# Linear attention, Fourier mixing and feed-forward in one kernel: the check's flag is loaded in the middle, and a PSUM layout is turned

## The chip, the cores and the metric

The kernel runs on one core of one Trainium2 chip. A time is the device time of one execution in microseconds; the number for a kernel is the median of its runs. Engines are named as in the profile: PE is TensorE (PEld its weight loads), DVE is VectorE, ACT is ScalarE, POOL is GpSimd, SP is SyncE. A "q" behind an engine's name marks an instruction of its sequencer (a wait, a branch, the issue of a transfer).

## The reference

Four batches, eight heads, 768 tokens, 48 features per head. First a gated linear attention, token by token, and then, on the heads side by side (384 features), a Fourier mixing over tokens and features, a normalization and a two-layer feed-forward with a residual:

```python
for t in range(S):
    state = alpha[:, :, t, :, None] * state + np.einsum('bhd,bhe->bhde', k[:, :, t], v[:, :, t])
    y[:, :, t] = np.einsum('bhd,bhde->bhe', q[:, :, t], state)
...
X = np.fft.fft(x, axis=1)
X = np.fft.fft(X, axis=2)
u = x + np.real(X)
un = (u - mean(u)) / np.sqrt(var(u) + 1e-06)
out = u + np.maximum(un @ w_ch1, 0.0) @ w_ch2
```

## The kernel before, in words

**Two paths.** The fast path works on chunks of 128 tokens and divides by running products of `alpha`. This needs products that stay in range, so it also makes a check: each pair of heads leaves a count in `bad` (ScalarE, stage `s1`) and six chunk products in `over`. At the end `lim`, `bs` and a one-column product on TensorE turn these into `fl`, an integer 0 or 1. A general path follows under `tc.If(flag > 0)` (line 1375): it computes the whole output again with a scan over each state column. With the inputs of the reference the flag is 0 and every engine jumps over it. Its code is large for some engines: `general_pair` and `general_rest` use PE, DVE, ACT and SP much, POOL little.

**The fast path's stages.** Each of the 16 pairs of heads (`attn_stages`, four pairs per batch) goes through `s1` to `s8`: two scans that make the running products and their inverses (`products`, which also copies the chunk products to `over` and to `fade_`), the multiplications with keys and queries, transposes of the keys (`s4`), scores (`s5`), the chunk states (`s6`), the output (`s7`) and the first step of the mixing (`s8`). In `s6` five chunks times two heads give ten products of 128x48 into one PSUM tile `pu`; VectorE multiplies them by the chunk products `mt` into `tc_`, where the chunk is the innermost index, a scan over the five chunks makes the states, and two ScalarE copies put them into `tt`. After four pairs comes the Fourier mixing of the batch: a token stage with twelve products per two groups (`token_stage`, which writes PSUM with a step of six), a feature stage, a gather through DRAM, and the normalization. The feed-forward (`ffn_stages`) has for each of two blocks of 384 tokens twelve slices, each with nine matmuls in and nine out, weights and data split into a high and a low part.

**What sets the order.** Nothing is emitted where it is written. Every instruction goes into a `Plan` (line 212) with a key (its due order), the engines that could do it (`FX`), and durations from `Plan.duration` (line 334). `Plan.emit` (line 398) places them greedily on modelled clocks and then emits the instructions in that order; almost all have line 530 in the profile (ScalarE's relu 249). Feed-forward matmuls have `fill` and take whatever time the others leave on TensorE. Where the plan leaves TensorE idle before the time `WARM`, `plan.idle` inserts dummy matmuls of 128x48 on `zero` (line 1284), one per 0.11 us of planned gap.

**The end of the program.** The check's instructions have the key `B * 1000`, behind everything. After `plan.emit()` line 1302 loads the flag into a register of every engine (`nc.values_load`), each waiting for `fl`; line 1375 is the branch, and line 1437 the close of the program, where SP waits for all engines and all transfers.

The input and output transfers of the fast path are issued by SP, two small ones by ACT, the gathers by POOL.

Of the kernel before, what the change touches and what calls it, by code (L numbers as in the profile page):

```python
# [17 lines left out]
ALU = mybir.AluOpType  # L18
AX = mybir.AxisListType

B, H, S, D = 4, 8, 768, 48
# [10 lines left out]
CW = 112  # L32
# [25 lines left out]
KFM = 40.0  # L58
WARM = 120.0
SWITCH = 0.09  # L60
# [151 lines left out]
class Plan:  # L212


    def __init__(self, engines):
        self.engines, self.ops, self.tags, self.direct, self.key, self.chain, self.fill = engines, [], {}, None, 0.0, None, False
        self.idle, self.open, self.both, self.half, self.tight = None, set(), None, None, False
        self.read = {}

# [33 lines left out]
    def add(self, engines, name, args, kwargs):  # L253
        engine = engines[0]
        fns = {e: self.method(e, name) for e in engines}
# [78 lines left out]
    def duration(self, op, named, engine):  # L334
        n = op.free
        if "dma" in op.name:
            return 1.05 if engine == "POOL" else 0.05
        if engine == "PE":
            m = self.region(named["1"])[4]
            if op.name == "transpose":  # L340
                return max(m, self.region(named["2"])[4]) / 1200 + 0.002
            if str(named["1"].real(self.base(named["1"])).dtype).endswith("float32"):
                slow = 1.65 if self.stride(named["2"]) > 16 else 1.0
                p0, p1 = self.region(named["1"])[0:2]
                return max(m, slow * n) / (750 if p1 - p0 <= GRP else 600) + 0.004
            return n / 2240 + 0.003
        if engine == "ACT":
            pointer = 0.094 if any(isinstance(named.get(k), View) for k in ("bias", "scale")) else 0.0
            slow = 1.8 if self.stride(named["out"]) > 16 and n > 64 else 1.0
            return (0.11 if self.psum(named.get("1")) else 0.14) + slow * n / 1200 + pointer + (0.25 if "accum_out" in named else 0.0)  # L350
        if op.name == "memset":
            return n / (960 if engine == "DVE" else 1100) + 0.01
        if engine == "DVE":
            if op.name == "bn_stats":
                return 0.47
            if op.name == "reciprocal":
                return 0.07 + n / 160
            if op.name == "tensor_tensor_scan":
                return 0.1 + n / 480
            if isinstance(named.get("scalar1"), View):  # L360
                return 0.09 + n / 1200
            whole = "bitcast" in [s[0] for s in named.get("out", View(None)).steps]
            pointer = 0.06 if isinstance(named.get("scalar"), View) else 0.0
            return 0.09 + pointer + n / (1920 if whole and op.name == "tensor_scalar" else 960)
        return 0.126 + n / 1094 if op.name == "affine_select" else 0.15 + n / 477

    def stride(self, view):

        ap = view.real(self.base(view))
        return abs(ap.ap[-1][0]) * mybir.dt.size(ap.dtype)  # L370

    def port(self, op, named):
# [25 lines left out]
    def emit(self):  # L398
# [33 lines left out]

        placed = 0
        while placed < len(ops):
# [32 lines left out]
            t, n, engine = best  # L467
            op = ops[n]
            for e in op.engines:
                wait[e].remove(n)  # L470
# [26 lines left out]
            if "dma" in op.name:  # L497
                dge = max(dge, t) + 0.47
                wire = max(wire, dge + 0.6) + op.wire * (1.4 if wire < 9.0 else 0.9)
                end = wire + 1.0  # L500
            op.t, op.end = t, end
            order.append(n)
            for slot in op.slots:
# [7 lines left out]
            for m in op.users:  # L511
                u = ops[m]
                u.left -= 1
                for e in u.engines:
# [4 lines left out]
                    if not u.left:  # L519
                        wait[e].append(m)  # L520
        self.order = [n for n in order if isinstance(n, int)]
        for n in order:
# [27 lines left out]
def gla_mix_ffn(ctx: ExitStack, tc: tile.TileContext, alpha, kq, v, w1, w2, consts, tables, rowtab, out):  # L550
# [172 lines left out]
    def attn_stages(b, hp, i, mixed):  # L723
# [83 lines left out]
        def s6():  # L807
            pu = psa()
            ea = tc_.rearrange("p (e a) -> p a e", a=NT - 1)
            for a in range(NT - 1):  # L810
                for hd, r in HEADS:
                    T.matmul(
                        pu[r, a * D : (a + 1) * D], e["kt"][:, a, r], loaded["vn", pair][:, (2 * a + hd) * D : (2 * a + hd + 1) * D],
                        start=True, stop=True,
                    )
            V.tensor_tensor(
                out=ea[0:CW], in0=pu[0:CW, 0 : (NT - 1) * D].rearrange("p (a e) -> p a e", e=D),
                in1=mt[0:CW, 0 : NT - 1, None].broadcast_to([CW, NT - 1, D]), op=ALU.mult,
            )
# [430 lines left out]
    for b in range(B):  # L1250
# [14 lines left out]
        if b + 1 < B:  # L1265
# [6 lines left out]
            write(mixing(), b * 1000 + KM)  # L1272
    plan.key = B * 1000.0
    lim, wide = bad[0:CW, B * NP2 :], over[0:CW]
# [4 lines left out]
    T.matmul(pf[0:1, 0:1], bs, ones, start=True, stop=True)  # L1279
    V.tensor_scalar_min(fl, pf[0:1, 0:1], 1.0)  # L1280
    warm = {tag: plan.tags[tag]["reals"] for tag in ("f2", "f1")}
    if WARM:
# [18 lines left out]
    plan.direct = own  # L1301
    flag = nc.values_load(fl.real()[0:1, 0:1], min_val=0, max_val=1)
    ydram = dp.tile([B * NP2, S, 2 * D], F32, name="ydram")
# [70 lines left out]

    with tc.If(flag > 0):
        with tc.tile_pool(name="gp", bufs=1) as pool:
# [64 lines left out]
```

## Time and profile before

| | |
|---|---|
| median of 3 runs | 508.88 us (508.25 to 509.34) |
| the profiled execution: its time | 508.06 us |
| its span, first to last instruction | 506.3 us |
| mean granted TensorE clock | 0.996 |
| HBM read, written | 37.69 MB, 7.08 MB |

A row of grouped instructions has line, engine, operation, out<-in by the program's names (buffer numbers left out), shapes and count, then busy time, mean ns of one, and the idle time of the engine before them with what ended it. A row of the timeline has start, duration, then the same. A row of one line's instructions has count, duration ns (minimum/median/maximum), and first and last start. The ends of matmuls are modelled, so rows of matmuls overlap.

### The profile page before, as it was taken

To read this page: it belongs to the slowest core of one execution; us is meant where nothing else is said; L and a number is where in the kernel's file an instruction comes from. 1 tells how busy PE (TensorE), PEld (TensorE's weight loads), DVE (VectorE), ACT (ScalarE), POOL (GpSimd) and SP (SyncE) were. 2 spreads that over 40 slices of the span, in tenths; PEclk is the share of its full clock that TensorE was granted. 3 is DMA by queue.
4 is the path that set the end of the run, shared out by engine and by line. 5 is a ranking of instruction groups with operands and counts; after the bars stand their busy time and mean duration, and the time that the engine had idled before them with its cause. 6 is when DMAs were issued, how large, how long until landed. Compare 5 with 4: busy or idle time off the path is not lost.

```text
span 506.3 us, 9559 instructions
## 1 busy us (share of the span) xinstructions
PE 495.9 (98%) x3956; PEld 472.8 (93%) x3956; DVE 322.6 (64%) x617; ACT 206.9 (41%) x417; POOL 61.9 (12%) x76
## 2 busy tenths in 40 slices
PE   9999999999999999999999999999999999999993
PEld 8888769999999999999999999999999999999993
DVE  8999989999789996561799516661648214113111
ACT  3494678576664164544323314445123312111110
POOL 0000250532113002121200002121300000000000
PEclk9999999999999999999999999999999999999998
DMA  8993442234532103322431001200201001001001
GB/s 304 407 403 130 117 138 92 95 88 176 212 109 81 47 1 141 117 91 89 141 104 48 0 1 48 87 26 2 79 18 47 1 1 47 1 0 48 0 1 53
DMA packets 20978, 45.47 MB, mean 90 GB/s; under 512 B 1920, under 2 KB 11008, under 8 KB 20928
## 3 DMA queue, kind: packets, MB, share of 16 engines
q1 hardware_dynamic: 19872, 42.29, 23.8%
q0 software_dynamic: 768, 2.37, 1.7%
q8 instruction: 33, 0.54, 0.5%
q10 hardware_dynamic: 288, 0.13, 0.1%
q14 instruction: 17, 0.14, 0.1%
HBM read 37.69 MB, written 7.08 MB: 88 GB/s over the span
## 4 chain that ended last, share of the span: by engine, by line
PE 96%; DVE 2%; issue 0%
PE f L530 68%; PE a L530 24%; PE f L1284 4%; DVE y L530 1%; DVE st L530 0%; DVE r L530 0%; DVE mv L530 0%; DVE f L530 0%; DVE x L530 0%; DVE zero L530 0%; DVE fl L530 0%
## 5 line engine op out<-in xcount | busy, mean ns | idle before, releaser
L530 PE MATMUL f<-x,wt 128*128 128x384 f32 x864 | 178.6, 343 | 0.6 <-DVE x L530 0.6
L530 PE MATMUL f<-wt,h 128*128 128x384 f32 x864 | 176.5, 343 | 0.0
L530 PEld LDWEIGHTS f<-x,wt 128*128 128x128 f32 x864 | 150.7, 188 | 1.9 <-DVE x L530 0.8
L530 PEld LDWEIGHTS f<-wt,h 128*128 128x128 f32 x864 | 151.2, 188 | 1.3 <-issue 0.5
L530 DVE SCALAR_TENSOR_TENSOR h<-f,h 128x384 fp32r<-128x384 f32 x96 | 53.2, 554 | 110.2 <-ACT h L249 109.6
L249 ACT ACTIVATE h<-f 128x384 fp32r<-128x384 f32 x96 | 47.2, 492 | 169.3 <-PE f L530 154.9
L530 POOL TENSOR_SCALAR_AFFINE_SELECT w<-w 128x384 f32<-128x384 f32 x48 | 34.7, 746 | 208.1 <-ACT w L530 207.9
L530 PE MATMUL a<-vn,w 128*128 128x80 f32 x288 | 42.6, 270 | 0.0
L530 PEld LDWEIGHTS a<-vn,w 128*128 128x128 f32 x288 | 39.6, 191 | 0.6
L530 ACT COPY w<-a 128x384 f32<-128x384 f32 (+4 forms) x60 | 26.4, 482 | 26.2 <-PE a L530 25.0
L530 DVE TENSOR_TENSOR y<-y,a 128x191 f32<-128x191 f32 (+3 forms) x65 | 25.1, 427 | 10.4 <-PE a L530 10.4
L530 DVE TENSOR_TENSOR_SCAN w<-al,d 112x773 f32<-112x773 f32 (+1 forms) x17 | 28.7, 1691 | 4.6 <-PE a L530 3.4
L530 DVE TENSOR_TENSOR_SCAN al<-al,back 112x773 f32<-112x773 f32 (+1 forms) x17 | 30.0, 1762 | 0.2
L1284 PE MATMUL f<-zero 128*32 128x48 f32 x518 | 27.8, 212 | 1.1 <-DVE zero L530 1.1
L1284 PEld LDWEIGHTS f<-zero 128*32 128x32 f32 x518 | 24.5, 114 | 4.4 <-issue 1.5
L530 ACT COPY tt<-tc 64x240 f32<-64x240 f32 (+1 forms) x32 | 20.5, 640 | 12.1 <-DVE tc L530 11.6
L530 PEld LDWEIGHTS a<-w,al 64*128 64x128 f32 (+1 forms) x288 | 17.9, 187 | 5.1 <-ACT w L530 2.5
L530 PE MATMUL a<-w,al 64*128 64x128 f32 (+1 forms) x288 | 22.5, 288 | 0.0
L530 DVE TENSOR_TENSOR z<-y,y 128x576 f32<-128x576 f32 x16 | 12.8, 832 | 15.2 <-ACT y L530 15.1
L530 POOL DMA_INDIRECT y<-scr,rows x12 | 15.4, 1285 | 56.8 <-DMA scr<-y 32.0
L530 PE MATMUL a<-tt,w 112*128 112x96 f32 x120 | 21.4, 276 | 0.0
L530 ACT COPY y<-a 128x288 f32<-128x288 f32 x24 | 9.6, 402 | 25.8 <-PE a L530 25.8
(113 smaller groups left out, 545.3 us busy)
## 6 DMA issues: line engine op xcount, KB each, us to landing
kq<-in_kq_dram SPq DMA_DIRECT2D x13, 768.0 KB, 5.5
wt<-in_w_dram SPq DMA_DIRECT2D x8, 768.0 KB, 8.4
al<-in_alpha_dram SPq DMA_DIRECT2D x15, 388.0 KB, 5.7
out_dram<-y SPq DMA_DIRECT2D x24, 192.0 KB, 2.3
vn<-in_v_dram SPq DMA_DIRECT2D x14, 304.0 KB, 3.0
wt<-in_w_dram SPq DMA_DIRECT2D x8, 384.0 KB, 6.5
scr<-y SPq DMA_DIRECT2D x4, 577.5 KB, 4.7
wt<-in_kq_dram SPq DMA_DIRECT2D x2, 768.0 KB, 11.7
```

Source lines behind the costliest of these rows:

```text
L249: return lambda out, x: e.activation(out, x, AF.Relu)
L530: op.ins = op.fns[op.engine](*[real(a) for a in op.args], **{k: real(x) for k, x in op.kwargs.items()})
L1284: lambda tag, i: nc.tensor.matmul(warm[tag][i][0:32, 512 - FW : 512], zero.real()[:, 0:32], zero.real(), start=True, stop=True), 1.0, WARM,
```

## The change

Four things. The check's instructions get a key that lies within batch 2's work (2430), behind the attention of the last batch, and `Plan.emit` emits the load of the flag for all engines at the first instruction placed more than 10 us of planned time after `fl` is planned to be done. In the general path (`self.direct`) what SP issued is issued by ACT. In `s6` the products are written with the chunk innermost, so that PSUM, the multiplication's other operand and `tc_` have the same order. And the planner's prices change: TensorE's for products with at most 64 weight columns on full rows, ScalarE's for inputs with a step over 16 bytes and for outputs with a last dimension under 8; `WARM` goes from 120 to 220.

```diff
-WARM = 120.0
+WARM = 220.0
...
     def add(self, engines, name, args, kwargs):
-        engine = engines[0]
+        engine = "ACT" if self.direct and engines[0] == "SP" else engines[0]
+        engines = (engine,) if self.direct else engines
...
+                if m <= GRP < p1 - p0:
+                    return max(m / 2, n) / 600 + 0.004
                 return max(m, slow * n) / (750 if p1 - p0 <= GRP else 600) + 0.004
...
-            slow = 1.8 if self.stride(named["out"]) > 16 and n > 64 else 1.0
+            apart = max(self.stride(named[k]) for k in ("out", "1") if isinstance(named.get(k), View)) > 16
+            slow = 1.8 if (apart or self.short(named["out"])) and n > 64 else 1.0
...
+    def short(self, view):
+        ap = view.real(self.base(view)).ap
+        return len(ap) > 2 and ap[-1][1] < 8
...
+            if due is not None and t > due:
+                order.append(self.after)
+                due = None
...
+            if n == self.last:
+                due = end + 10.0
...
-                        pu[r, a * D : (a + 1) * D], e["kt"][:, a, r], loaded["vn", pair][:, (2 * a + hd) * D : (2 * a + hd + 1) * D],
+                        pu[r, a : (NT - 1) * D : NT - 1], e["kt"][:, a, r], loaded["vn", pair][:, (2 * a + hd) * D : (2 * a + hd + 1) * D],
...
-                out=ea[0:CW], in0=pu[0:CW, 0 : (NT - 1) * D].rearrange("p (a e) -> p a e", e=D),
-                in1=mt[0:CW, 0 : NT - 1, None].broadcast_to([CW, NT - 1, D]), op=ALU.mult,
+                out=tc_[0:CW].rearrange("p (e a) -> p e a", a=NT - 1), in0=pu[0:CW, 0 : (NT - 1) * D].rearrange("p (e a) -> p e a", a=NT - 1),
+                in1=mt[0:CW, None, 0 : NT - 1].broadcast_to([CW, D, NT - 1]), op=ALU.mult,
...
-    plan.key = B * 1000.0
+    plan.key = (B - 2) * 1000.0 + KA + 10.0
...
+    flag = []
+    plan.last = len(plan.ops) - 1
+    plan.after = lambda: flag.append(nc.values_load(fl.real()[0:1, 0:1], min_val=0, max_val=1))
...
-    flag = nc.values_load(fl.real()[0:1, 0:1], min_val=0, max_val=1)
...
-    with tc.If(flag > 0):
+    with tc.If(flag[0] > 0):
```

More of the change, by code (lines that the diff above doesn't have):

```diff
@@ L217, in __init__ @@
         self.idle, self.open, self.both, self.half, self.tight = None, set(), None, None, False
-        self.read = {}
+        self.read, self.last, self.after = {}, None, None
     def tag(self, name, count, make):
@@ L431, in finish @@
             return (max(t, held[other[e]]) if op.port and e in held else t) + op.durs[e]
-        placed = 0
+        placed, due = 0, None
         while placed < len(ops):
@@ L520, in emit @@
                         wait[e].append(m)
+        if due is not None:
+            order.append(self.after)
         self.order = [n for n in order if isinstance(n, int)]
```

## The prediction

> **What bounds the kernel now.** I read the page's totals first, then windows over four stretches, the end of the timeline, the sequencers' rows behind it, and last the groups that the change touches.
>
> ```profile
> span 506.3 us, 9559 instructions
> PE 495.9 (98%) x3956; PEld 472.8 (93%) x3956; DVE 322.6 (64%) x617; ACT 206.9 (41%) x417; POOL 61.9 (12%) x76
> PE 96%; DVE 2%; issue 0%
> ```
>
> TensorE carries 96% of the chain that ended last, but that averages over stages. Here are the windows (PE, PEld, DVE, ACT, POOL, then clock, DMA share, GB/s), and the dummy matmuls of line 1284 with their first and last start:
>
> ```profile
> 10.00:60.00 50.00, 49.49 (x572) 42.05 (x573) 48.52 (x82) 30.41 (x55) 3.64 (x3) 1.00 0.73 281
> 80.00:120.00 40.00, 40.00 (x317) 38.10 (x315) 37.94 (x55) 27.89 (x56) 10.91 (x9) 1.00 0.18 59
> 120.00:220.00 100.00, 100.00 (x781) 96.48 (x779) 80.19 (x149) 49.94 (x104) 15.04 (x20) 1.00 0.33 112
> 220.00:498.00 278.00, 278.00 (x1909) 272.30 (x1909) 130.11 (x275) 80.47 (x171) 22.43 (x31) 1.00 0.12 40
> L1284 PE MATMUL f<-zero x518: 206/206/288, 1.1 to 77.0; 128*32 128x48 f32 x173
> ```
>
> So there are three stages. Until 77 us TensorE is padded with dummies, and VectorE is the full engine (48.52 of 50 us between 10 and 60), with DMA at 0.73 beside it. From 80 to 498 us TensorE never stops: only a change in its own work counts there. The third stage is the end:
>
> ```profile
> 497.59 1.61 DVE L530 TENSOR_TENSOR y<-y,f 128x384 f32<-128x384 f32 x3 [1.03 <-PE f L530]
> 498.54 0.09 PEld L530 LDWEIGHTS a<-ones,bs 128*1 128x1 f32 x2 [0.25 <-issue]
> 498.54 0.19 PE L530 MATMUL a<-ones,bs 128*1 128x1 f32 x2
> 499.12 0.14 DVE L530 TENSOR_SCALAR fl<-a 1x1 int32<-1x1 f32 x1
> ```
>
> The last addition ends at 497.59 + 1.61 = 499.20 us, yet the span runs to 506.3. After the flag (499.26) no engine is busy; the sequencers' rows (q behind the engine; first and last start) show what is there:
>
> ```profile
> L1302 PEldq TENSOR_LOAD <-fl x1: 662/662/662, 499.3 to 499.3; - x1
> L1302 SPq TENSOR_LOAD <-fl x1: 981/981/981, 500.1 to 500.1; - x1
> L1375 SPq EVENT_SEMAPHORE  x8: 17/17/17, 504.1 to 504.7; - x8
> L1375 POOLq EVENT_SEMAPHORE  x2: 17/30/43, 500.2 to 500.3; - x2
> L1375 POOLq COMPARE_BRANCH  x1: 45/45/45, 500.0 to 500.0; - x1
> L1375 PEldq COMPARE_BRANCH  x1: 4462/4462/4462, 500.1 to 500.1; - x1
> L1375 SPq COMPARE_BRANCH  x1: 45/45/45, 501.5 to 501.5; - x1
> L1375 DVEq EVENT_SEMAPHORE  x1: 21/21/21, 503.6 to 503.6; - x1
> L1375 PEldq EVENT_SEMAPHORE  x1: 51/51/51, 504.6 to 504.6; - x1
> L1437 SPq EVENT_SEMAPHORE  x14: 17/28/28, 504.7 to 506.3; - x14
> L530 SPq DMA_DIRECT2D out_dram<-y x3: 534/575/582, 498.2 to 499.5; - x3
> DMA to landing us min/median/max: 2.2/2.4/2.7
> ```
>
> Every engine loads the flag after it is made (499.3), then jumps over the general path. The jump is long on engines with much code there: PE's takes 4.46 us, SP goes from its branch at 501.5 to its next instruction at 504.1 (2.6 us), DVE goes on at 503.6. POOL, with little code there, takes 0.2 us (500.0 to 500.2). SP comes last: its load stands behind its output transfers (500.1 to 501.1), then the branch, then eight releases from 504.1 to 504.7, and the closing run to 506.3. The last two rows say that the third output transfer starts at 499.5, keeps SP 0.58 us, and that these three land 2.4 us after their issue.
>
> **The tail, after the change.** The flag is made and loaded long before, so nobody loads at the end. SP has no transfers of the general path left (ScalarE has them), so I give its jump POOL's 0.2 us. The third output transfer lands at 499.5 + 2.4 = 501.9; SP, past its jump at 500.3, waits for that. From the last release to the end is 506.3 - 504.7 = 1.6 us; the landing is awaited somewhere among eight releases that take 0.6 us, so I add 0.3: the end is 501.9 + 1.6 + 0.3 = 503.8, a gain of 2.5 us. With the landing at its shortest, 2.2 us, and awaited last, the gain is 3.0. If SP's jump stays at 2.6 us, SP goes on at 500.1 + 2.6 = 502.7 instead of 504.1, and 1.4 us are gained.
>
> PE's 4.46 us jump must not become the end. Does PE's sequencer reach it early? A wait in the first stage answers:
>
> ```profile
> L530 PEldq EVENT_SEMAPHORE  x1: 2257/2257/2257, 26.7 to 26.7; - x1
> 27.38 1.34 PE L530 MATMUL f<-vn,x 128*128 128x80 f32 x10
> 28.65 0.27 PE L1284 MATMUL f<-zero 128*32 128x48 f32 x2
> ```
>
> From 26.7 to 29.0 PE's sequencer stood still while the array ran ten matmuls and two dummies that had been queued before. So it runs some 2 us ahead: it meets the branch 2 us before the last matmuls (498.5 - 2 = 496.5) and is through by 501.0, ahead of the landing. ScalarE's last work lies earlier than that. VectorE's 3.6 us (500.0 to 503.6), started no later than 499.2, ends by 502.8, about when SP asks for it. If PE did not run ahead, its jump would end at 498.7 + 4.5 = 503.2, and with the 1.7 us from there (504.6 to 506.3) the end would be 504.9: a gain of 1.4.
>
> **The flag inside the feed-forward.**
>
> ```profile
> L530 DVE TENSOR_SCALAR bad<-over x1: 407/407/407, 326.5 to 326.5; 112x96 f32<-112x96 f32 x1
> L530 DVE TENSOR_REDUCE bs<-bad x1: 270/270/270, 332.1 to 332.1; 128x1 f32<-128x112 f32 x1
> ```
>
> The sums were made at 326 to 332 us already; their new key changes little. What moves is the one-column product, the flag, and five loads. The product's two matmuls now stand in TensorE's full stretch: 0.19 us, or 0.44 with the 0.25 of issue that preceded them; I take 0.25. Behind it on PE wait feed-forward matmuls, and behind those the output. The load blocks PE's sequencer for 0.66 us; by the wait above the array has some 2 us queued, so it costs nothing. Without that cover it costs 0.66. On ACT, DVE and SP, loads of 0.65 to 0.98 us fall into a stretch where VectorE is busy 130 of 278 us: nothing, at worst the same 0.66 once. The queues passed on SP hold only transfers; POOL is idle.
>
> **Keys' products, chunk innermost.**
>
> ```profile
> L530 DVE TENSOR_TENSOR tc<-a,over 112x240 f32<-112x240 f32 x12 | 7.2, 598 | 17.6 <-PE a L530 17.6
> L530 DVE TENSOR_TENSOR tc<-f,over 112x240 f32<-112x240 f32 x4 | 2.3, 585 | 0.1
> L530 DVE TENSOR_TENSOR y<-y,a 128x191 f32<-128x191 f32 x36 | 11.2, 343 | 0.0
> L530 DVE TENSOR_TENSOR y<-y,a 128x384 f32<-128x384 f32 x24 | 12.7, 546 | 10.4 <-PE a L530 10.4
> 29.03 0.75 PE L530 MATMUL f<-wt,kt 128*64 128x48 f32 x20
> 26.35 0.60 PE L530 MATMUL f<-cst,al 112*128 112x112 f32 x4
> 60.31 2.68 PE L530 MATMUL f<-cst,h 128*97 128x65 f32 x24
> ```
>
> The multiplication wrote with a step of five and took 585 to 598 ns for 240 elements. Two others that read PSUM without such a step take 343 for 191 and 546 for 384, so 1.05 ns per element and 343 + 49 x 1.05 = 394 for 240: 0.2 us less, 16 times, 3.2 us of VectorE. Only the first four can shorten the time, in the stage where VectorE is full: at most 4 x 0.19 = 0.76. The matmuls that now write with a step of five (20 bytes) are the twenty of 0.75 us per pair. The token stage already writes with a step of six: twelve products (641 and 640 columns) in two passes each, 2562 columns in 2.68 us, 1.05 ns per column; four contiguous transposes, 448 columns in 0.60, are no faster. So I take nothing. As the upper bound, if the step held the keys' 960 columns to 1.05 ns each, though two heads now run beside each other, the twenty would take 1.0 us: 0.25 more, 3.0 for the twelve pairs in the full stretch.
>
> The Trainium skill, PSUM — Partial Sum Buffer, section Specifications (TRN2), speaks against this edit: it says that any non-contiguous access pattern in PSUM slows matmuls significantly. It gives no factor, and the token stage's row does not bear it out.
>
> **The planner's new prices.**
>
> ```profile
> L530 ACT COPY fade<-w 112x192 f32<-112x192 f32 x11 | 5.9, 540 | 0.0
> L530 DVE COPY fade<-w 112x192 f32<-112x192 f32 x4 | 1.4, 362 | 0.0
> ```
>
> They move no work by themselves, but the order is made anew. Dearer ScalarE copies may send some fades to VectorE: 0.36 us each, up to three more in the first stage, 1.1 us against the 0.76 saved. I take -0.3 for both together, from -0.8 to +1.1. In the full stretch the order can only cost stalls or save few: nothing, plus or minus 0.8. The dummies up to 220: before, none came after 77 us although 120 was allowed, so the plan had no gaps there; nothing, at most ten (10 x 0.05 = 0.5 us, since 518 took 27.8). The transfers issued by ScalarE are never run.
>
> **Sum**, on the profiled execution (span 506.3, its own time 508.06): tail -2.5, product +0.25, loads 0, matmuls' step 0, first stage -0.3, order and dummies 0: -2.55, so 505.5. The median of the runs, 508.88, lies 0.82 above that execution; the same -2.55 on it gives 506.3.
>
> **Rivals.**
>
> *Half the tail (chance 0.12).* SP's jump stays long, because what Tile itself puts on SP for the general path's loops is more than POOL's share; or the load is not hidden. A tail of 1.4 in place of 2.5 gives 507.4; a load of 0.66 on TensorE, 507.0; both, 508.1. For it: SP had 2.6 us, and no row shows how much of that was transfers. Against it: POOL has the same loops and jumps in 0.2. The Trainium skill, Runtime: NRT & Kernel Launch, section Instruction fetch mechanics, says that a taken branch stalls for a fetch only when its target lies outside the blocks already loaded; by it SP's rest must fit such a block, which no row here shows.
>
> *Nothing (0.07).* Something not seen, such as the code fetches themselves, sets the end wherever the flag is: 508.9. Against it: POOL's short jump at the same time.
>
> *Slower, by the new order in the first stage (0.10).* The first feed-forward matmul, near 77 us, waits for a chain through a full VectorE. If the new prices put another pair's two scans and a product ahead of it, everything behind moves:
>
> ```profile
> L530 DVE TENSOR_TENSOR_SCAN al<-al,back 112x773 f32<-112x773 f32 x15 | 28.0, 1869 | 0.1
> L530 DVE TENSOR_TENSOR al<-kq,al 112x768 f32<-112x768 f32 x13 | 12.3, 945 | 1.9 <-DMA kq<-in_kq_dram 1.9
> ```
>
> Two scans and one product are 4.7 us: 506.3 + 4.7 = 511.0. It decides from a delay of 2.6 us on. For it: VectorE has no slack there. Against it: the new prices are nearer to the measured ones (540 ns for the fade).
>
> *Slower, by the step in PSUM (0.05).* If the keys' matmuls take twice as long, the twelve pairs in the full stretch cost 12 x 0.75 = 9 us: 515.3. It decides from 1.3 times on.
>
> **How the numbers follow.** A measurement of this kernel can tell 0.2%, 1.0 us, from no change. The forecast has 0.66 and by its terms runs from 504.8 to 507.6. The range goes on to 508.9 and takes in half the tail and nothing; the two slower cases, 0.15, stay out. Faster by over 1.0 us: nearly all of the forecast, 0.63, and two thirds of half the tail, 0.08: 0.71. Slower: 0.05 and most of the other, 0.08: 0.13. The rest, 0.16, is the same.
>
> **What would show it.** Right: no load of the flag after the last matmul; PE's branch starting before its last matmul; SP's next instruction within 0.3 us of its branch; the last addition followed by 4.6 us (503.8 - 499.2) and not 7.1; the multiplication near 394 ns; the first feed-forward matmul within 1 us of 77. Wrong: a gap in PE's weight loads at the flag's load, dummies after 80 us, keys' twenty matmuls over 0.9 us, or SP's jump still at 2.6.

## The result, and the profile after

The changed kernel takes 513.63 us (median of 6 runs, 510.43 to 514.13) where the kernel before takes 508.94 (6 runs beside it, 508.25 to 509.34): ratio 1.0084, 95% interval 1.0057 to 1.011. It is slower by 4.7 us, and the forecast of 506.3 missed by 7.3.

The profiled execution took 513.36 us. Its span:

```profile
span 511.6 us, 9570 instructions
```

The windows over the same four stretches as before:

```profile
10.00:60.00 50.00, 49.82 (x573) 42.48 (x571) 44.52 (x76) 29.37 (x55) 2.46 (x2) 1.00 0.73 281
80.00:120.00 40.00, 40.00 (x318) 37.49 (x317) 38.41 (x60) 27.57 (x57) 11.12 (x9) 0.98 0.25 83
120.00:220.00 100.00, 99.23 (x766) 95.24 (x766) 78.94 (x146) 49.55 (x100) 14.34 (x20) 1.00 0.30 101
220.00:498.00 278.00, 277.97 (x1921) 272.13 (x1921) 133.77 (x280) 83.48 (x178) 23.11 (x33) 1.00 0.13 44
```

TensorE is as full as before, VectorE has less to do between 10 and 60 us (44.52 us, 48.52 before), and the stretch from 120 us on lacks little: one idle time of 0.8 us between 120 and 220. So the loss must lie at an end of the program. The last addition is the place to cut (timeline of after, its end):

```profile
503.69 1.61 DVE L545 TENSOR_TENSOR y<-y,f 128x384 f32<-128x384 f32 x3 [1.04 <-PE f L545]
```

It ends at 503.69 + 1.61 = 505.30 and ended at 499.20: 6.10 us later. From there to the end of the span it is 6.34 us instead of 7.14. So the tail gained 0.80, and 6.10 were lost ahead of it. The profile of before, around the first feed-forward matmul (f<-x,wt), first on GpSimd, then on VectorE, then on TensorE:

```profile
61.18 0.95 POOL L530 DMA_INDIRECT y<-scr,rows  x1 [0.30 <-issue]
66.01 3.60 POOL L530 TENSOR_TENSOR wt<-wt 128x768 f32<-128x768 f32 x2 [3.88 <-ACT wt L530]
69.57 3.61 POOL L530 TENSOR_TENSOR wt<-wt,wt 128x768 fp32r<-128x768 f32 x2
...
71.97 1.22 DVE L530 SCALAR_TENSOR_TENSOR r<-mv,r 128x3 f32<-128x3 f32 x1
...
73.82 0.48 DVE L530 TENSOR_SCALAR f<-y,r,r 128x384 f32<-128x384 f32 x1
...
74.64 1.20 PE L530 MATMUL f<-cst,f 128*128 128x128 f32 x9 [0.63 <-ACT f L530]
...
76.40 0.44 PE L530 MATMUL f<-x,wt 128*128 128x384 f32 x1
```

The same place in after:

```profile
63.49 4.69 POOL L545 DMA_INDIRECT y<-scr,rows  x1 [0.30 <-issue]
68.20 1.83 POOL L545 TENSOR_TENSOR wt<-wt,wt 128x768 fp32r<-128x768 f32 x1
69.97 3.59 POOL L545 TENSOR_TENSOR wt<-wt 128x768 f32<-128x768 f32 x2
73.50 3.58 POOL L545 TENSOR_TENSOR wt<-wt,wt 128x768 fp32r<-128x768 f32 x2
...
72.76 0.52 DVE L545 TENSOR_TENSOR y<-y,a 128x384 f32<-128x384 f32 x1
73.20 0.17 DVE L545 RECIPROCAL r<-r 128x3 f32<-128x3 f32 x1
73.42 3.69 DVE L545 SCALAR_TENSOR_TENSOR r<-mv,r 128x3 f32<-128x3 f32 x1
...
77.73 0.48 DVE L545 TENSOR_SCALAR f<-y,r,r 128x384 f32<-128x384 f32 x1
...
78.55 2.18 PE L545 MATMUL f<-cst,f 128*128 128x128 f32 x9 [3.09 <-ACT f L545]
80.67 1.17 PE L1302 MATMUL f<-zero 128*32 128x48 f32 x12
81.77 0.44 PE L545 MATMUL f<-x,wt 128*128 128x384 f32 x1
```

The first feed-forward starts at 81.77 instead of 76.40, 5.37 later, and three differences make that up. The three-element instruction r<-mv,r starts 73.42 - 71.97 = 1.45 later. It then takes 3.69 us instead of 1.22, 2.47 more, and ends (77.11) where GpSimd's last pair of subtractions ends (77.08); in before it ended (73.19) where that pair ended too (73.18). And from f<-y,r,r to the first matmul it is 4.04 instead of 2.58, 1.46 more, because nine transposes take 2.18 instead of 1.20 and twelve dummies 1.17 instead of 0.70, after TensorE had been idle for 3.09 us. The granted clock, the first of the last three numbers, was 0.79 there:

```profile
76.00:84.00 8.00, 5.45 (x36) 4.75 (x37) 7.86 (x19) 3.58 (x7) 1.08 (x1) 0.79 0.74 246
```

The first of the three is no loss by the new order: the start varies. In the profile of `after_dummies`, below, whose order is the same up to there, the same instruction starts at 72.32, and with the prices of before, in `after_oldprices`, at 73.30. The difference arises in the first 9 us: the first transposes (f<-cst,al) start at 7.76 in before, 9.14 in after and 8.05 in `after_dummies`.

Now the tail of after. The branch's line, with first and last start, then the close of the program, and the last three output transfers:

```profile
L1392 SPq EVENT_SEMAPHORE  x8: 17/17/17, 506.8 to 510.0; - x8
...
L1392 PEldq COMPARE_BRANCH  x1: 3431/3431/3431, 502.7 to 502.7; - x1
...
L1392 SPq COMPARE_BRANCH  x1: 45/45/45, 506.3 to 506.3; - x1
```

```profile
L1454 SPq EVENT_SEMAPHORE  x14: 17/28/28, 510.0 to 511.6; - x14
```

```profile
L545 SPq DMA_DIRECT2D out_dram<-y x3: 534/584/644, 504.3 to 505.6; - x3
...
DMA to landing us min/median/max: 2.7/3.2/4.0
```

PE's branch starts some 1.6 us before the last matmul does (504.37). SP's jump is short, 506.3 to 506.8. What SP then waits for is the landing: 505.6 + 4.0 = 509.6, the last release at 510.0, and 1.6 to the end.

Finally the flag's load on PE, and the multiplication and the keys' matmuls by their groups:

```profile
L1298 PEldq TENSOR_LOAD <-fl x1: 764/764/764, 366.5 to 366.5; - x1
```

```profile
L545 DVE TENSOR_TENSOR tc<-a,over 112x240 f32<-112x240 f32 x12 | 4.7, 392 | 10.2 <-PE a L545 10.2
L545 PE MATMUL a<-vn,kt 128*64 128x48 f32 x120 | 9.4, 226 | 0.0
```

The load stands where TensorE does not stop; the multiplication takes 392 ns; the keys' products take the 226 ns that they took before.

### The profile page after: what moved, and what is told of

Read it like the earlier page. It is cut to its first block, busy times and chain, and to the rows that moved or that the text cites. A ratio compares the mean times of both kernels' runs of the same rounds, so it can differ in the third digit from the quotient of the medians.

```text
span 511.6 us, 9570 instructions
## 1 busy us (share of the span) xinstructions
PE 499.6 (98%) x3966; PEld 476.2 (93%) x3966; DVE 324.0 (63%) x616; ACT 207.2 (40%) x416; POOL 68.3 (13%) x78
## 4 chain that ended last, share of the span: by engine, by line
PE 97%; DVE 2%; issue 0%; ACT 0%; ACTq 0%
PE f L545 68%; PE a L545 24%; PE f L1302 5%; DVE r L545 1%; DVE y L545 1%; DVE st L545 0%; ACT f L545 0%; DVE mv L545 0%; DVE zero L545 0%; ACTq L545 0%
## 5 line engine op out<-in xcount | busy, mean ns | idle before, releaser
L545 POOL TENSOR_SCALAR_AFFINE_SELECT w<-w 128x384 f32<-128x384 f32 x48 | 32.4, 698 | 198.0 <-ACT w L545 198.0
L1302 PEld LDWEIGHTS f<-zero 128*32 128x32 f32 x528 | 26.6, 119 | 4.4 <-issue 1.6
L1302 PE MATMUL f<-zero 128*32 128x48 f32 x528 | 29.7, 219 | 1.0 <-DVE zero L545 1.0
L545 POOL DMA_INDIRECT y<-scr,rows x12 | 19.2, 1596 | 51.0 <-DMA scr<-y 26.1
L545 DVE TENSOR_TENSOR z<-y,y 128x576 f32<-128x576 f32 x16 | 11.6, 751 | 15.9 <-ACT y L545 15.9
```

What stands on the lines that cost most here:

```text
L545: op.ins = op.fns[op.engine](*[real(a) for a in op.args], **{k: real(x) for k, x in op.kwargs.items()})
L1302: lambda tag, i: nc.tensor.matmul(warm[tag][i][0:32, 512 - FW : 512], zero.real()[:, 0:32], zero.real(), start=True, stop=True), 1.0, WARM,
```

## The experiments

The theory after the result: the new prices make another order ahead of the first feed-forward, in which GpSimd's subtractions of the weights end later and hold VectorE; and the jumps' code fetches, now at the same time as the last output transfers, take the rest of the tail's gain. The rivals: the step in PSUM, the loads of the flag, or the mere new order on VectorE.

### One part of the change at a time

**prices_only**: before with the new `duration()` alone.

```diff
+                if m <= GRP < p1 - p0:
+                    return max(m / 2, n) / 600 + 0.004
...
-            slow = 1.8 if self.stride(named["out"]) > 16 and n > 64 else 1.0
+            apart = max(self.stride(named[k]) for k in ("out", "1") if isinstance(named.get(k), View)) > 16
+            slow = 1.8 if (apart or self.short(named["out"])) and n > 64 else 1.0
```

> Only the planner's new prices on the kernel before. Theory A (the order made from the new prices puts more of GpSimd's weight work into the first normalization, where VectorE then waits; the first feed-forward matmul comes at 81.8 instead of 76.4 us): slower by 4 to 6 us, 513 to 515, first feed-forward matmul after 80 us, one three-element VectorE instruction near 3.7 us. Rival B (the flag's product and load, or the matmuls' step in PSUM, cost the time): within 1 us of before, 508.0 to 509.9.

Measured: 511.48 (511.27 to 513.51), ratio 1.006 (1.004 to 1.0079). Its rows on GpSimd and TensorE, and then the window from 76 to 84 us, with the clock behind the five engines:

```profile
62.47 4.68 POOL L537 DMA_INDIRECT y<-scr,rows  x1 [0.30 <-issue]
72.49 3.56 POOL L537 TENSOR_TENSOR wt<-wt,wt 128x768 fp32r<-128x768 f32 x2
...
77.52 1.20 PE L537 MATMUL f<-cst,f 128*128 128x128 f32 x9 [3.10 <-ACT f L537]
```

```profile
76.00:84.00 8.00, 5.84 (x47) 5.29 (x48) 7.86 (x24) 4.82 (x10) 0.05 (x1) 1.00 0.64 236
```

The prices alone cost 2.5 us, less than the 4 to 6 expected: they bring the same long gather, the same late pair, and the same idle time of 3.1 us, but here the clock stayed at 1.00.

**layout_only**: before with the turned layout of `s6` alone (three edits, as in the change).

```diff
-                        pu[r, a * D : (a + 1) * D], e["kt"][:, a, r], loaded["vn", pair][:, (2 * a + hd) * D : (2 * a + hd + 1) * D],
+                        pu[r, a : (NT - 1) * D : NT - 1], e["kt"][:, a, r], loaded["vn", pair][:, (2 * a + hd) * D : (2 * a + hd + 1) * D],
```

> Only the keys' products with the chunk innermost; every engine's order is that of before. Theory A: the multiplication takes 395 ns instead of 590 and the time falls by 0 to 0.8 us, 508.1 to 508.9. Rival B (the step in PSUM slows the keys' matmuls): slower by 3 us or more, 512 and above, the twenty matmuls over 1 us.

Measured: 509.01 (508.52 to 510.14), ratio 1.0 (0.9991 to 1.001). The order of every engine stays; nothing is gained or lost.

**flag_only**: before with the early flag and the general path's transfers on ScalarE, old prices and layout.

```diff
-    plan.key = B * 1000.0
+    plan.key = (B - 2) * 1000.0 + KA + 10.0
...
+    plan.after = lambda: flag.append(nc.values_load(fl.real()[0:1, 0:1], min_val=0, max_val=1))
```

> Only the flag: made and loaded in the middle, general path's transfers from ScalarE; PE's order differs by the product and the load alone. Theory A: the tail shrinks from 7.1 us after the last addition to 6.3, and the product and load cost TensorE at most 0.3: 508.0 to 508.6, faster by 0.3 to 0.9. Rival B (the load costs TensorE's queue): slower by 0.5 or more.

Measured: 507.86 (506.66 to 508.82), ratio 0.9974 (0.9963 to 0.9985). 1.2 us are gained, not the 2.25 that the forecast has for this part (tail 2.5 less 0.25 for the product): its last outputs land 3.2 to 3.6 us after issue.

**after_oldprices**: the whole change, with the prices and `WARM` of before.

```diff
-WARM = 220.0
+WARM = 120.0
...
-                if m <= GRP < p1 - p0:
-                    return max(m / 2, n) / 600 + 0.004
...
-            slow = 1.8 if (apart or self.short(named["out"])) and n > 64 else 1.0
+            slow = 1.8 if self.stride(named["out"]) > 16 and n > 64 else 1.0
```

> The whole change with the prices of before (and the dummies up to 120, which changes no order): flag and layout together. Theory A: sum of the two, 507.3 to 508.4. Rival B: as slow as the changed kernel, 512 to 514.

Measured: 507.44 (506.45 to 508.61), ratio 0.997 (0.9956 to 0.9983). GpSimd's last pair and the three-element instruction:

```profile
70.90 3.59 POOL L542 TENSOR_TENSOR wt<-wt,wt 128x768 fp32r<-128x768 f32 x2
...
73.30 1.21 DVE L542 SCALAR_TENSOR_TENSOR r<-mv,r 128x3 f32<-128x3 f32 x1
```

So the prices turn a gain of 1.6 us into a loss of 4.7. The instruction starts as late as in after, and ends with GpSimd's pair again (74.51 and 74.49).

### What holds VectorE's three elements

**after_short_pool**: GpSimd's multiplications of the weights cover 8 columns, and its subtractions of the weights become memsets. This leaves out the low parts of some weights.

```diff
+            if op.engine == "POOL" and op.name == "tensor_sub":
+                op.ins = self.engines["POOL"].memset(real(op.args[0]).bitcast(I32), 0)
+                continue
+            args = op.args
+            if op.engine == "POOL" and op.name == "tensor_mul":
+                args = [x[..., 0:8] for x in args]
```

> The changed kernel with GpSimd's weight work cut down: its multiplications cover 8 columns and its subtractions are memsets, so the low parts of some weights are left out; the order is kept. Theory A (GpSimd's two-operand work holds VectorE's three-element instruction in the first normalization): that instruction falls from 3.7 us to about 0.2, the first feed-forward matmul comes 3 us or more earlier (78 to 79), time 508 to 510.5. Rival B (the instruction waits for something else): still 3.7 us and 513 to 514.

Measured: 507.01 (505.89 to 508.26), ratio 0.9958 (0.9941 to 0.9974).

```profile
73.36 0.16 DVE L551 SCALAR_TENSOR_TENSOR r<-mv,r 128x3 f32<-128x3 f32 x1
...
77.28 0.45 PE L551 MATMUL f<-x,wt 128*128 128x384 f32 x1
```

The instruction starts at the same time and takes 0.16 us; the first feed-forward comes 4.5 us earlier than in after, and the time is 6.6 us lower. The order is that of the new prices. The gather is as long as in after (4.68 us). So it is GpSimd's work on the weights beside it, and not VectorE's own order, that costs.

**after_pause**: eight memsets of 128x64 on VectorE, behind the first copy of 385 columns.

```diff
+            if op.engine == "DVE" and op.name == "copy" and op.free == 385 and self.pause is not None:
+                for _ in range(8):
+                    self.engines["DVE"].memset(self.pause.real(), 0.0)
+                self.pause = None
```

> The changed kernel with eight small VectorE memsets (about 0.7 us in all) put behind the copy that precedes the weights' shifts; every other order is kept. Theory A (VectorE's unbroken run of instructions with two SBUF operands keeps GpSimd from finishing its third gather: 4.69 us instead of 0.95, and GpSimd's weight work, now late, then holds VectorE's small instruction for 3.7 us): the third gather falls to about 1 us, the small instruction to under 2 us, first feed-forward matmul 1.5 to 3 us earlier (79 to 80), time 509.5 to 512. Rival B (the gather is long for its own reasons, its DRAM side or its descriptors): gather still over 4 us, time unchanged or 0.7 us longer, 513 to 515.

Measured: 512.25 (510.59 to 514.23), ratio 1.0074 (1.0056 to 1.0092). A miss: there are two such copies, and the memsets fell behind the one at 48 us. The gather stayed at 4.69 us, so this run says nothing of what makes it long.

**after_pause2**: the same memsets behind the second copy.

```diff
+            if op.engine == "DVE" and op.name == "copy" and op.free == 385 and self.pauses.pop():
+                for _ in range(8):
+                    self.engines["DVE"].memset(self.pause.real(), 0.0)
```

> The whole change, with eight memsets of 128x64 float32 (by the rows of VectorE's small memsets together some 1 us or less) put on VectorE behind the second copy of 385 columns, which is where the third gather on GpSimd stood in the trace of after; the other engines' orders stay. Theory A (the third gather takes 4.69 us instead of 0.95 because VectorE keeps working without a gap beside it, and the weights' subtractions on GpSimd are late by that): a stretch in which VectorE writes without reading lets the gather finish in 1 to 2 us, the subtractions end some 3 us earlier, the three-element instruction r<-mv,r takes under 2 us, the first feed-forward starts 1.5 to 3 us earlier than 81.8; time 509.5 to 512. Rival B (the gather's length belongs to the gather's own data or place on its queue): it stays over 4 us, and the time is 513 to 515.

Measured: 512.47 (511.21 to 513.48), ratio 1.0063 (1.0049 to 1.0077). GpSimd, then VectorE:

```profile
63.67 0.95 POOL L545 DMA_INDIRECT y<-scr,rows  x1 [0.31 <-issue]
68.18 2.47 POOL L545 TENSOR_TENSOR wt<-wt,wt 128x768 fp32r<-128x768 f32 x1 [3.56 <-ACT wt L545]
74.16 3.58 POOL L545 TENSOR_TENSOR wt<-wt,wt 128x768 fp32r<-128x768 f32 x2
...
74.25 3.51 DVE L545 SCALAR_TENSOR_TENSOR r<-r,r 128x3 f32<-128x3 f32 x2
```

Half of the theory holds and half falls. The gather is back at 0.95 us beside VectorE's memsets, so its length came from what VectorE did at that time. But GpSimd then waits for ScalarE's weights until 68.18, as late as the gather had ended: the memsets (1.45 us together) delayed the chain through ScalarE by as much as the gather gave back. The last pair ends at 77.74, and what is held this time is the next instruction, r<-r,r: two of three elements take 3.51 us, to 77.76.

**after_sub_dve**: the one subtraction with which GpSimd starts (68.20 in after) is emitted for VectorE, where the old prices have it.

```diff
+        order.insert(j + 1, order.pop(i))
+        sub.fns["POOL"] = sub.fns["DVE"]
```

(`i` is the place of that subtraction, `j` that of the ScalarE copy that it reads.)

> The whole change with the new prices, and one single instruction moved: the subtraction of 128x768 with which GpSimd starts behind its third gather (68.20 us in the trace of after, 1.83 us) is emitted for VectorE, between its two int32 instructions of 128x768, where the old prices have it; the order of all else stays. Theory A (VectorE's instruction of three elements with two SBUF operands is held until GpSimd's last two weight subtractions end, and these are late by the sum of the extra subtraction and the long gather): the gather stays near 4.7 us, GpSimd's last pair ends near 75.3 instead of 77.1, the held instruction gets shorter by some 1.5 us, first feed-forward near 80, time 511.5 to 512.5. If the extra subtraction alone is the cause (the gather's length is nobody's), the last pair ends near 74.5, first feed-forward near 79, time 510 to 511.5. Rival B (the hold has nothing to do with GpSimd's work): unchanged, 513 to 514.

Measured: 512.72 (510.21 to 514.45), ratio 1.0075 (1.005 to 1.0101). Its last pair on GpSimd, and VectorE's small instructions:

```profile
73.53 3.58 POOL L550 TENSOR_TENSOR wt<-wt,wt 128x768 fp32r<-128x768 f32 x2 [0.88 <-ACT wt L550]
...
73.90 1.48 DVE L550 SCALAR_TENSOR_TENSOR r<-mv,r 128x3 f32<-128x3 f32 x1
75.41 1.92 DVE L550 SCALAR_TENSOR_TENSOR r<-r,r 128x3 f32<-128x3 f32 x2
```

The pair starts where it did in after, and holds VectorE about as long (the last of the small ones starts at 77.37, 77.54 in after), but in two pieces: VectorE gets in between the two subtractions. GpSimd had been free earlier (its first multiplication started at 67.26), but beside that multiplication VectorE's last two int32 instructions took 2.56 us (1.81 in after), ScalarE's work on their results came later, and GpSimd stood idle for 1.77 and 0.88 us before its next instructions. So neither of the two delays alone sets the pair's end: in these two attempts the chain from VectorE over ScalarE to GpSimd came last at about the same time instead.

**after_subs_dve**: in addition, the last two subtractions go to VectorE. Nothing is left out.

```diff
+        for n in [n for n in order if isinstance(n, int) and ops[n].engine == "POOL" and ops[n].name == "tensor_sub"][1:3]:
+            ops[n].fns["POOL"] = ops[n].fns["DVE"]
```

> As the run before, and the two last weight subtractions on GpSimd (73.50 to 77.08 us in the trace of after) are emitted for VectorE as well, where they fall behind the first normalization's product f<-y,r,r; the two multiplications of the weights stay on GpSimd. Nothing is left out. Theory A: GpSimd is idle from about 72 us, the three-element instruction takes 0.2 us as soon as it is reached (its place near 74 us), but VectorE carries three subtractions of 0.95 us more, two of them ahead of x<-f,x, so the first feed-forward starts 1 to 4 us earlier than 81.8; time 510 to 513. Rival B: the hold stays at over 3 us, first feed-forward at 82 or later, time over 513.

Measured: 511.84 (510.72 to 513.24), ratio 1.0068 (1.0055 to 1.0081).

```profile
73.03 0.16 DVE L552 SCALAR_TENSOR_TENSOR r<-mv,r 128x3 f32<-128x3 f32 x1
...
79.51 4.78 PE L552 MATMUL f<-x,wt 128*128 128x384 f32 x17 [1.97 <-DVE x L552]
```

The hold is gone as soon as GpSimd has no subtraction there, and the first feed-forward matmul comes at 76.73. But VectorE pays for it: its own subtractions come ahead of x<-f,x, so TensorE waits 1.97 us after the first matmul, and the next seventeen run at a lowered clock (0.86 as a mean from 72 to 84 us).

**after_novg** and **oldprices_novg**: the weights' splits planned on VectorE alone, once with the new prices and once with the old (`'wm': 'V', 'wd': 'V'` in `FX`, order planned anew).

> The whole change with the new prices, but the splits of the weights may only be planned on VectorE, so that GpSimd has no two-operand work beside the first normalization; the order is planned anew. Theory A (the 5 us come from GpSimd's paired work that holds VectorE's small instruction): the instruction takes under 0.5 us and TensorE has no 3 us of idle before the first feed-forward, while VectorE carries some 2 to 4 us more of its own; time 507 to 511, below after's 513.6. Rival B (the new order of VectorE's work itself is what is late): 513 or more.

> The whole change with the prices of before (507.4 with GpSimd's share of the splits), and the splits planned on VectorE alone. Theory A: the three-element instruction goes from 1.2 us to some 0.2, and up to 1 us is gained, less what VectorE's added splits delay: 506 to 508.5. Rival B (GpSimd's share relieves VectorE by more than it holds it): 508.5 to 511.

Measured: 509.52 (508.88 to 510.28), ratio 1.001 (1.0001 to 1.0018); and 507.07 (506.64 to 509.22), ratio 0.9964 (0.9952 to 0.9977). With the new prices this wins back 4.1 of the 4.7 us: the three-element instruction takes 0.16 us and the first feed-forward starts at 75.91, 5.9 earlier than in after, though 1.3 of this is an earlier start of that instruction (72.16 instead of 73.42), and the stretch from there to the last matmul is 2.9 longer. With the old prices GpSimd's share makes no difference that these runs can tell (507.07 beside 507.44); there the pair ends early enough to hold only 1.2 us.

### The clock

**after_dummies**: the whole change with 60 more dummy matmuls before the first normalization's transposes, to fill the idle 3.1 us.

```diff
+            if op.name == "transpose" and op.args[1].tile.tag == "f" and self.fills:
+                self.fills = False
+                bank = min((x for x in self.idle[3] if x not in self.open), key=lambda x: self.read.get(x, 0.0))
+                order.extend([lambda bank=bank: self.idle[0](*bank)] * 60)
```

> The changed kernel with 60 more dummy matmuls ahead of the first normalization's transposes, where TensorE idles for 3.1 us. Theory A's second part (that gap lowers the granted clock to 0.8 for some 8 us, which costs 1.5 to 2 us in most runs): granted clock 1.0 from 76 to 88, time 511 to 512.2, the runs closer together. Rival B (the clock costs nothing beside the delay): 513 to 514.

Measured: 511.71 (511.0 to 513.15), ratio 1.0062 (1.0045 to 1.0079). The granted clock stays at 1.00, the nine transposes take 1.17 us instead of 2.18, and the median is 1.9 below after's; the ranges of the two overlap, so the size is rough. The dummies also cost something: they run until 79.47, and the transposes start 2.95 us behind f<-y,r,r (76.67 to 79.62), where it was 0.82 in after (77.73 to 78.55). So some 2.1 us of what the clock gives are spent again, and the run alone does not price the clock.

The single runs say more. Of after's six, the one with a mean granted clock of 0.997 took 510.43 us, and the five with 0.989 to 0.994 took 512.84 to 514.13. Of the six of `prices_only`, the four with 0.996 or 0.997 took 511.27 to 511.52, and the two with 0.994 took 513.27 and 513.51. The runs of `after_pause` and `after_sub_dve` divide in the same way: 510.21 to 511.52 from 0.996 on, 512.00 to 514.45 up to 0.994, and one of 512.51 at 0.995. (The mean holds the end of the program too, where TensorE is idle: the profile of `after_novg` has 0.995 with no fall ahead of it.) So the medians of after and of `prices_only` come from different groups.

The five profiles with an idle time of about 3.1 us fall apart by the start. Where the first transposes start at 8.1 us (`prices_only`, `after_pause`), TensorE is idle from 74.4 to 77.5 and the clock stays at 1.00. Where they start at 8.9 to 9.3 (after, `after_pause2`, `after_sub_dve`), it is idle from 75.3 to 75.6 on, until 78.4 to 78.8, and the clock falls (0.79 as a mean from 76 to 84). Why the place matters is not shown.

### The tail

**flag_nogen**: `flag_only` without the general path and its branch, which this kernel leaves out.

```diff
-    with tc.If(flag[0] > 0):
...
```

> The flag's part alone, with the general path and its branch left out. Theory A (the engines' code fetches behind their jumps now fall onto the last output transfers and hold them up): the three transfers land 2.2 to 2.5 us after issue instead of 3.2 to 4.0, the tail falls from 6.0 us to 4.3 to 4.8, time 506 to 507. Rival B (the transfers land late for another reason): landing stays at 3 to 4 us and the tail at 5.5 or more.

Measured: 505.85 (504.97 to 506.23), ratio 0.9936 (0.9921 to 0.995). Its last outputs:

```profile
DMA to landing us min/median/max: 2.2/2.3/2.4
```

In after, the DMA view from 504.2 to 509.8 us, between the first issue and the landing, has code on two queues beside the outputs:

```profile
q1 hardware_dynamic: 816, 0.59, 33.4%
q8 instruction: 1, 0.02, 1.7%
q14 instruction: 4, 0.03, 1.6%
```

In before, no code is fetched until 501.5 us, when the outputs' packets are nearly through (the last one starts at 501.6). In `flag_nogen` no code is fetched at that time at all, and the longest landing is 2.4 us instead of 3.6 in `flag_only`. The path that is never taken still costs 2.0 us; by the two profiles the tail is 2.2 us shorter, some 1.3 of it by the landing and the rest by the waits behind it.

The traces also show which of the code costs most. In after the packet of q8 starts at 506.9 us and takes some 1.5 us (an estimate: 1.7% of 16 engines' 5.6 us); no output packet starts between 508.08 and 508.34, and the last 16 follow behind it. In all five profiles where q8's packet comes that early (after, `flag_only`, `after_short_pool`, `after_novg`, `oldprices_novg`), the last 16 output packets start only as it ends, and the longest landing is 3.6 to 4.3 us. In the seven others with the early branch it starts within 0.4 us of the outputs' end, and the longest landing is 3.1 or 3.2 us.

**flag_sp**: `flag_only`, with the general path's transfers left on SP.

```diff
-        engine = "ACT" if self.direct and engines[0] == "SP" else engines[0]
+        engine = engines[0]
```

> The early flag alone (507.9 with the general path's transfers issued by ScalarE), with these transfers left on SyncE's queue, so that SyncE jumps over its own general path's instructions. Theory A (the length of a jump is set by the code that it goes over): SyncE's jump takes some 2.6 us as before instead of 0.5, and SyncE releases the output later by up to 1 us: 508 to 509. Rival B (its jump is short because it comes early, not because it is short code): 507.5 to 508.

Measured: 508.21 (507.74 to 508.62), ratio 0.9982 (0.9973 to 0.9991). The branch's line in it, and after that in `flag_only`:

```profile
L1389 SPq EVENT_SEMAPHORE  x8: 17/17/17, 504.5 to 505.1; - x8
...
L1389 SPq COMPARE_BRANCH  x1: 45/45/45, 501.6 to 501.6; - x1
```

```profile
L1389 SPq EVENT_SEMAPHORE  x8: 17/17/17, 502.2 to 505.0; - x8
...
L1389 SPq COMPARE_BRANCH  x1: 45/45/45, 501.7 to 501.7; - x1
```

SP's jump is 2.9 us with its own transfers to jump over and 0.5 without, so the code sets its length. But the last release comes at 505.1 or 505.0: behind the short jump SP waits for the outputs until then. The part of the change that moves transfers to ScalarE buys at most 0.35 us, and the intervals of the two overlap.

## Why the prediction was wrong, point by point

**The planner's new prices: the step that failed.** The prediction said that the prices "move no work by themselves" and counted fades, from -0.8 to +1.1 us in the first stage. It did not ask what else the new order puts beside the first normalization. One more subtraction went to GpSimd, the third gather got long, and GpSimd's last pair, which held VectorE for 1.22 us in before already, held it for 3.69. The chain of work that ended last in before lists the hold already (start and duration; the next ones on `r` take 0.17):

```profile
71.97 1.24 DVE r L530
```

The runs put numbers on it: the prices alone +2.5; on top of the rest 513.63 instead of 507.44, +6.2. By the profiles of these two, 4.05 of a span 5.7 longer lie ahead of the first feed-forward (81.77 and 77.72), 2.5 of them by the hold and 1.5 by the clock behind the idle time; the tail has 1.2, the full stretch the other 0.5. Only the hold comes with the new prices in every profile that keeps their order and GpSimd's work; the clock and the landing go by where things fall in time. So much of the step from 2.5 to 6.2 is no property of the order: after's run with the clock at 0.997 lost 1.5 us against before, not 4.7.

The rival of a slower first stage (0.10) had the place and the sign, and 511.0 against 513.63. Its mechanism, two more scans on VectorE, is not what happened: with the same order and GpSimd's work made short, the kernel is faster than before.

The Trainium skill has the mechanism, in SBUF — State Buffer, section Who interferes with whom: a VectorE instruction with two SBUF inputs contends with a GpSimd instruction that reads SBUF, and whichever issues first has the shared ports for its whole instruction, while the other is blocked. The trace agrees in which instructions are held: r<-mv,r is (3.69 us), while the reciprocal with one input (0.17) and y<-y,a, whose `a` lies in PSUM (0.52), run beside GpSimd untouched. It goes further in length: 3.69 us are two of GpSimd's instructions back to back, not one. In `after_sub_dve` VectorE got in between the two (1.48 us, then 1.92); what decides that is open.

**The tail: right in direction, a third of its size.** 2.5 us were forecast and 0.80 came in after's profile (0.6 to 2.0 in the twelve profiles with the early branch). Three of its terms held: no loads at the end, PE's jump hidden by its run-ahead (branch 1.6 us ahead of the last matmul, 2 forecast), SP's jump short (0.5, 0.2 forecast). The term that was mis-sized is the landing: 2.4 us taken from before, the median of a row whose longest is 2.7; 4.0 measured (3.1 in `after_oldprices`, 3.6 in `flag_only`). In before the jumps' code arrived behind the outputs; the early branch put both at the same time. The 1.6 us missing there are the difference, as 505.6 + 4.0 + 0.4 + 1.6 gives the span's 511.6. That the landing varies among kernels with the same code goes by where q8's packet falls; what places it is open.

**The flag inside the feed-forward: right.** The load of 764 ns on PE stops no matmul, the product's two matmuls take 0.19 us (0.25 forecast), and the median of `flag_only` is below before.

**Keys' products: right for the matmuls, and the saving was worth nothing.** 392 ns against 394 forecast, matmuls unchanged at 226 ns, ratio of the layout alone 1.0 (0.9991 to 1.001). The Trainium skill's rule on non-contiguous patterns (PSUM — Partial Sum Buffer, Specifications (TRN2)), which spoke against it, did not show with this step of five. The four shortened multiplications of the first stage, 0.76 us at most, shorten nothing that is last.

**Order and dummies: small, but not nothing.** Ten more dummies, as bounded, none after 82.4 us. The full stretch has one idle time of 0.8 us on TensorE that before lacks; its cause is open.

**What stays open.** The shares of the long gather and of the extra subtraction in GpSimd's delay: by after's rows the multiplications start 69.97 - 67.34 = 2.63 later than in `after_oldprices`, and the subtraction takes 1.83 of that, but each attempt to take one of the two away let the chain over ScalarE come last. And why an idle time of 3.1 us lowers the clock at one place and not a microsecond earlier.

**A version that beats both**: the change without its new prices, 507.44 us, or with the splits kept off GpSimd as well, 507.07. The runs don't tell these two apart.

## What to carry to other kernels

A change to a planner's prices is a change to the whole order: before trusting it, look in the profile of before for instructions that take far longer than their like (1.22 us beside 0.16), for they can show where two engines block each other, as here, and a shift of either can make the block longer. When an action is moved earlier, ask what then runs beside it: the jumps' code fetches, harmless behind the outputs, were put on top of them. And take the parts of a compound change one at a time: here one part lost more than the other two gained. Where the runs of one kernel lie in two groups, look at what divides them before a median is explained.

## What the runs showed of the hardware that was not expected

- A three-element VectorE instruction with two SBUF operands took 0.16, 1.2 or 3.7 us, by how long GpSimd's 768-column subtractions beside it still had to run; once, in `after_sub_dve`, it got in between two of them (1.48 us).
- An indirect gather on GpSimd took 0.95 us or 4.69 us, by what VectorE did meanwhile: 4.69 beside its back-to-back arithmetic on the weights, 0.95 beside memsets.
- TensorE's granted clock fell (0.86 as a mean from 72 to 84 us) after an idle time of 3.09 us in after and of 1.97 us in `after_subs_dve`; in `prices_only` and `after_pause` 3.10 and 3.11 us, a microsecond earlier in the program, left it at 1.00.
- A jump over code that is never run took 0.5 to 2.9 us on SP and 3.4 to 4.5 us on PE, and where its code arrived beside the last output transfers, the longest of these took 3.1 to 4.3 us to land, instead of 2.4 without that code. A single code packet of some 1.5 us kept the last 16 output packets waiting.
